# Linear attention and a maxout feed-forward: six of nine gate chunks in pairs by one level of Strassen

## The chip, the cores and the metric

The kernel runs on one core of a Trainium2 chip. The metric is the device time in microseconds (us) of that core; several executions are taken and their median is compared. The kernel before takes 719.25 us (median of 3 runs, 716.79 to 720.8).

The engines are TensorE (PE in the profile), VectorE (DVE), ScalarE (ACT), GpSimd (POOL) and SyncE (SP). Each runs its own instructions in order, and semaphores tie them together. SP only issues DMAs here; ACT issues a few as well.

## What is computed

q, k and v are (8, 8, 576, 64) in float32; x has 4608 rows (8 x 576 tokens) of 512 features (8 heads x 64). w1, w2 and w3 are 512 x 768 and w_out is 768 x 512, handed over as float64.

```python
q_s = exp(q - max(q, -1));  q_s = q_s / (sum(q_s, -1) + 1e-09)   # over a head's 64 features
k_s = exp(k - max(k, 2));   k_s = k_s / (sum(k_s, 2) + 1e-09)    # over the 576 tokens
kv = einsum('bhsd,bhse->bhde', k_s, v)
x  = einsum('bhsd,bhde->bhse', q_s, kv)      # then (tokens, 512)
h  = maximum(maximum(x @ w1, x @ w2), x @ w3)   # the gate product
out = h @ w_out                                 # the second product
```

## The kernel before

**Two parts of each number.** A product of two float32 matrices is made on PE from numbers cut into a high part (type float32r) and a low part, the remainder: high by high, high by low and low by high, three matmuls into one PSUM bank. Weights, x and the hidden layer h each exist in two parts: `wh` and `wl`, slot 0 and 1 of `xbuf`, `h_h` and `h_l`, `oh` and `ol` for w_out.

**Weights.** They come as 64-bit words and are joined to float32 on chip, 24 slices of 128 x 512 (`Slice`): load L332 into a slot `wst`, bit work on DVE (L344 to L351), a POOL addition (L355), the high part by ACT (L363), the low part by DVE or POOL (L370). A slot comes free when its low part is done.

**Heads.** One `Pair` is two heads of one batch (32 pairs). In batches 0 and 1 ("turned") q and k are transposed by PE, and x is one float32 matmul. In batches 2 to 7 q is read with rows in another order, normalised by DVE and ACT (L580 to L595), transposed in blocks by DVE (L600) and laid out by eight small DMAs on SP (L613), then cut in two parts (L619 ACT, L622 DVE). k's maximum is taken by three DVE steps (L481 to L483) and one POOL reduction (L486), then subtracted (L489) and exponentiated (ACT L496); k v is ten small matmuls (L511). Its block-diagonal matrix is written in two parts (`bdh` ACT L527, `bdl` DVE L531). x of a head pair (L663) is then three matmuls of 512 columns, and three of 64 columns for the last 64 tokens; its two parts are written by ACT (L666) and DVE (L668).

**Chunks.** Each batch's first 512 tokens are a chunk, and the eight last 64s together (`left`) a ninth. For a chunk the gate product (L693) is 18 groups (6 tiles j of 128 hidden features, 3 weights i) of 12 matmuls of 512 columns: 4 blocks of 128 features by the 3 terms, 216 in all, into 4 rotating PSUM banks (`pf`). After each group ACT copies it (L702) or DVE takes the maximum (L705); then h is cut in two (ACT L708, DVE L712). The second product (L732) is 4 groups of 18 matmuls; ACT copies each out (L750), SP stores it (L757). Heads' transposes and x use three banks `pa` and a bank of quarters `ps`.

**Order.** A planner (`Streams`) writes the order of every engine's instructions before the program is built: each piece of work is a chain of `Step`s with a cost, a rank, what it waits for and what rooms it takes and frees; the planner always issues the step that can begin first, by rank among those. The program then runs in this order on each engine.

Of the kernel before, what the change touches and what calls it, by code (L numbers as in the profile page):

```python
# [12 lines left out]
I32 = mybir.dt.int32  # L13
# [29 lines left out]
Q_BY_ACT = (0, 4, 6)  # L43

# [35 lines left out]
class Streams:  # L80
# [3 lines left out]
    def __init__(self, rooms, queued):  # L84
        self.all, self.when, self.blocked, self.left = [], {}, {}, 0
        self.queued = queued
        self.rooms = rooms
        self.taken = {}
        self.freed = {}
        self.clock = {"S": 0.72, "A": 2.2, "V": 4.0, "G": 9.0, "T": 0.0, "-": 0.0}  # L90
        self.port = 0.0
        self.queues = 0.0

    def add(self, gen, rank, inc=0.0):
        self.all.append([gen, rank, inc, 0.0, None, None])

    def ready(self, s, engine):
        step = s[4]
        lat = SIGNAL + (AHEAD if engine == "T" else 0.0)
        if engine == "-":  # L100
            t = s[3]
        elif s[5] != engine:
            t = s[3] + lat
        else:
            t = s[3] + 0.08 if engine not in "ST" else 0.0
# [6 lines left out]
        for r, key in step.take:  # L112
# [3 lines left out]
            if len(taken) >= self.rooms[r]:  # L116
# [52 lines left out]
    def issue(self, t, e, c, s):  # L169
# [9 lines left out]
        s[3], s[5] = end, e  # L179
# [5 lines left out]
        for r, key in step.take:  # L185
            self.taken.setdefault(r, []).append(key)
        for f in step.free:
            self.freed[f] = end
        s[1] += s[2]
# [6 lines left out]
def linear_attention_then_maxout_ffn(  # L196
# [46 lines left out]
    hp = ctx.enter_context(tc.tile_pool(name="hp", bufs=NJ))  # L243
    tmp = ctx.enter_context(tc.tile_pool(name="tmp", bufs=3))
    pf = ctx.enter_context(tc.tile_pool(name="pf", bufs=4, space=PSUM))
    pa = ctx.enter_context(tc.tile_pool(name="pa", bufs=3, space=PSUM))
# [4 lines left out]
    wh = [const.tile([P, NC, DF], F32R, name=f"wh{i}") for i in range(3)]  # L251
    wl = [const.tile([P, NC, DF], F32R, name=f"wl{i}") for i in range(3)]
    wo = []
    left = const.tile([P, 2, NC, B * LEFT], F32R, name="left")
    xbuf = [const.tile([P, 2, NC, CH], F32R, name="x0")]
# [5 lines left out]
    bdh, bdl = [], []  # L261
# [36 lines left out]

    in_pf = []
    for c in range(B + 1):  # L300
        in_pf += [(c, j, i) for j in range(NJ) for i in range(3)] + [(c, "y", t) for t in range(4)]
    st = Streams({"pf": 4, "pa": 3, "ps": 4, "keT": 1, "hp": NJ, "tmp": 3, "ke": 2, "qe": 2, "qf": 1, "qt": 2, "tb": 1, "qT": 2, "qhl": 1}, {"pf": in_pf})
    late_pools, turn_pools = [], []
# [6 lines left out]
    class Slice:  # L310


        def __init__(self, n):
            self.n = n
            if n < NG:
                j, i = divmod(n, 3)
                js = slice(j * P, (j + 1) * P)
                self.src = (w1, w2, w3)[i].bitcast(U32)[:, 2 * j * P : 2 * (j + 1) * P].rearrange("(c p) n -> p c n", p=P)
                self.parts = lambda: (wh[i][:, :, js], wl[i][:, :, js])
# [16 lines left out]
        def join(self, room):  # L336
# [17 lines left out]
            yield Step("G", 1.43, [("low", n)], gives=("w", n), port="G")  # L354
            nc.gpsimd.tensor_add(out=low.bitcast(I32), in0=x.bitcast(I32), in1=low.bitcast(I32))  # L355
# [9 lines left out]
        def lo(self, room):  # L365
# [4 lines left out]
            unit[e].tensor_sub(out=lo, in0=self.view(self.low.bitcast(F32)), in1=h.bitcast(F32))  # L370
# [3 lines left out]
    class Pair:  # L374
# [59 lines left out]
        def k_turned(self):  # L434
# [4 lines left out]
            kT = pa.tile([P, CH], F32, name="pa")  # L439
# [22 lines left out]
            kep = pa.tile([P, CH], F32, name="pa")  # L462
# [35 lines left out]
        def k_steps(self):  # L498
# [25 lines left out]
            yield Step("A", 0.65, free=last if turned else (), gives=("bd", n) if turned else None)  # L524
            for r in heads:
                to = (bdf if turned else bdh)[self.m]
                nc.scalar.activation(out=to[r, r], in_=kv[r, 0:D], func=AF.Copy, scale=rk[r])  # L527
            if not turned:
                yield Step("V", 0.45, free=last, gives=("bd", n))
                for r in heads:  # L530
                    nc.vector.scalar_tensor_tensor(  # L531
                        out=bdl[self.m][r, r],
                        in0=kv[r, 0:D],
                        scalar=rk[r],
                        in1=bdh[self.m][r, r].bitcast(F32),
                        op0=ALU.mult,
                        op1=ALU.subtract,
                    )


        def q_steps(self):
# [61 lines left out]
            for i in range(P // BL):  # L603
                for e in range(2):
                    end = i == P // BL - 1 and e == 1
                    yield Step(
                        "S", 0.6, take=[("qT", n)] if i == e == 0 else (), free=[("tb", n)] if end else (),
                        gives=("qT", n) if end else None, kb=36,
                    )
                    if i == e == 0:  # L610
                        self.qT = turn_pools[0].tile([P, S], F32, name="qT", bufs=2)
                    r = D * (i // 2) + BL * e
                    nc.sync.dma_start(  # L613
# [3 lines left out]
            yield Step("A", act(S), [("qT", n)], take=[("qhl", n)])  # L617
            q_h = turn_pools[0].tile([P, S], F32R, name="q_h", bufs=1)
            nc.scalar.copy(out=q_h, in_=self.qT)  # L619
            yield Step("V", dve(S), free=[("qT", n)], gives=("qhl", n), port="V")  # L620
            q_l = turn_pools[0].tile([P, S], F32R, name="q_l", bufs=1)
            nc.vector.tensor_sub(out=q_l, in0=self.qT, in1=q_h.bitcast(F32))  # L622
            self.terms = [(bdh[self.m], q_l), (bdl[self.m], q_h), (bdh[self.m], q_h)]

        def x_place(self, u):
            if u == 0:
                return tuple(xbuf[self.b % 2][:, i, self.g, :] for i in range(2))
            return tuple(left[:, i, self.g, self.b * LEFT : (self.b + 1) * LEFT] for i in range(2))

        def turned_steps(self):  # L630
# [3 lines left out]
            qT = pa.tile([P, CH], F32, name="pa")  # L634
# [11 lines left out]
            yield Step("A", act(LEFT), free=[("ps", ("qTl", n))], gives=("qhl", n))  # L646
            nc.scalar.copy(out=qf[:, CH:], in_=qTl[:, :LEFT])
            self.terms = [(bdf[self.m], qf)]

        def x_steps(self, u):  # L650
# [4 lines left out]
            cost = f32(w) if self.turned else 3 * f32r(w)  # L655
            after = [("bd", n), ("qhl", n), ("xmm", n, 0) if u else None]
            if u == 0:
                after += [("gates", b - 2) if b >= 2 else None, "late" if b == 1 else None]
            yield Step("T", cost, after, take=[room], gives=("xmm", n, u), free=[("qf" if self.turned else "qhl", n)] if u else ())
            xT = (next(small) if u else pa.tile([P, CH], F32, name="pa"))[:, :w]  # L660
            last = len(self.terms) - 1
            for i, (l, r) in enumerate(self.terms):
                nc.tensor.matmul(out=xT, lhsT=l, rhs=r[:, cs], start=(i == 0), stop=(i == last))  # L663
            h, lo = self.x_place(u)
            yield Step("A", act(w))
            nc.scalar.copy(out=h, in_=xT)  # L666
            yield Step("V", dve(w), free=[room], gives=("x", b, self.g) if u == 0 else ("xl", b, self.g))
# [4 lines left out]
    class Chunk:  # L672
# [6 lines left out]
        def gate(self, j, i):  # L679
            c, js = self.c, slice(j * P, (j + 1) * P)  # L680
            key = (c, j, i)
            for cc in range(NC):
                x = [("x", c, cc)] if c < B else [("xl", b, cc) for b in range(B)]
                yield Step(
                    "T", 3 * f32r(CH), [("split", 3 * j + i), *x], take=[("pf", key)] if cc == 0 else (),
                    gives=("gate", c, j, i) if cc == NC - 1 else None,
                )
                if cc == 0:
                    ps = pf.tile([P, CH], F32, name="pf")
                src = xbuf[c % 2] if c < B else left  # L690
                h, lo = src[:, 0, cc, :], src[:, 1, cc, :]
                for t, (l, r) in enumerate(((wl[i], h), (wh[i], lo), (wh[i], h))):
                    nc.tensor.matmul(  # L693
                        out=ps, lhsT=l[:, cc, js], rhs=r, start=(cc == 0 and t == 0), stop=(cc == NC - 1 and t == 2)
# [3 lines left out]
        def hidden(self, j):  # L698
# [8 lines left out]
            h = self.hh[j] = hp.tile([P, CH], F32R, name="h_h")  # L707
# [216 lines left out]
```

## Time and profile before

| | |
|---|---|
| median of 3 runs | 719.25 us (716.79 to 720.8) |
| profiled execution, span | 716.9 us |
| PE | busy 687.5 us, 3528 matmuls |
| DVE | busy 410.7 us, 819 instructions |
| ACT | busy 245.3 us, 529 instructions |
| POOL | busy 56.2 us, 70 instructions |
| DMA | 58.06 MB, mean 81 GB/s |
| HBM | 40.89 MB read, 9.44 MB written |
| L693, gate product | 1152 matmuls with a weight's high part and 576 with its low part in chunks 0 to 7; the ninth chunk's 216 have groups of their own |
| SP's longest wait | L757 for ACT at L750: 134.3 us in total, 9 times |

The profiled execution's span is 716.9 us; that is the time which the prediction's sum is made against, and the median stands 2.35 us above it. A row of the costliest groups reads: line, engine, operation, what is written and read, sizes, type, count, then busy time, mean ns of one, and idle time of the engine before them with what ended it. "PEld" is the loading of the stationary operand, which overlaps matmuls. In a row of the chain of waits stand start, length, engine, tile, line and count; in a row of the timeline start and length, then the instruction. Matmuls are pipelined, so that the mean of one overlaps its neighbours; the price of a matmul in a stream is the length of a stretch over its count.

### The profile page before, as it was taken

How to read it: one execution, taken by the hardware profiler on the slowest of the kernel's cores; microseconds unless marked ns; L12 is line 12 of the kernel's file. 1: busy time of each engine (PE TensorE's matmuls, PEld its weight loads, DVE VectorE, ACT ScalarE, POOL GpSimd, SP SyncE). 2: the span in 40 equal slices, each digit the busy share in tenths (PEclk: the TensorE clock that was granted, in tenths of full speed). 3: DMA queues.
4: the chain of work that ended last, by engine and by line, in shares of the span. 5: the costliest groups of instructions: out<-in, count | busy, mean ns of one | idle time of the engine just before them, and what ended most of it. 6: DMA issues, size and time to landing. Idle time of an engine off the chain costs nothing.

```text
span 716.9 us, 9773 instructions
## 1 busy us (share of the span) xinstructions
PE 687.5 (96%) x3528; PEld 553.2 (77%) x3528; DVE 410.7 (57%) x819; ACT 245.3 (34%) x529; POOL 56.2 (8%) x70
## 2 busy tenths in 40 slices
PE   2868999999999999999999999999999999999997
PEld 1536887778888888888888888887888888888885
DVE  7977978489996987785478546653422112211220
ACT  4677746433443334421342135113411111111111
POOL 3222332100000000000000001000000000000000
PEclk9959999999999999999999999999999999999999
DMA  9945713414453333530253015200200010010002
GB/s 232 246 129 160 218 46 106 125 29 121 117 155 102 99 93 101 148 85 17 59 152 98 16 43 160 76 13 26 84 1 0 16 45 0 1 44 16 1 0 59
DMA packets 86416, 58.06 MB, mean 81 GB/s; under 512 B 53344, under 2 KB 77920, under 8 KB 86368
## 3 DMA queue, kind: packets, MB, share of 16 engines
q1 hardware_dynamic: 86288, 57.31, 29.1%
q8 instruction: 28, 0.46, 0.3%
q14 instruction: 20, 0.16, 0.1%
q10 hardware_dynamic: 80, 0.13, 0.0%
HBM read 40.89 MB, written 9.44 MB: 70 GB/s over the span
## 4 chain that ended last, share of the span: by engine, by line
PE 92%; DVE 4%; DMA 2%; issue 1%; ACT 1%; SPq 1%; DVEq 0%; ACTq 0%
PE pf L693 62%; PE pf L732 21%; PE pa L663 3%; PE ps L511 3%; DMA wst<-in_moe_w_dram 2%; PE ps L663 1%; PE pa L636 1%; DVE wx L351 0%; DVE wx L346 0%; DVE wl L370 0%; PE pa L464 0%; SPq L795 0%; DVE km L450 0%; DVE qm L550 0%; DVE wx L347 0%
## 5 line engine op out<-in xcount | busy, mean ns | idle before, releaser
L693 PE MATMUL pf<-x,wh 128*128 128x512 f32 x1152 | 358.2, 392 | 0.0
L693 PEld LDWEIGHTS pf<-x,wh 128*128 128x128 f32 x1152 | 217.8, 189 | 46.4 <-issue 0.5
L693 PE MATMUL pf<-x,wl 128*128 128x512 f32 x576 | 230.3, 400 | 1.2 <-DVE wl L370 1.2
L705 DVE TENSOR_TENSOR m<-pf,m 128x512 f32<-128x512 f32 x108 | 74.6, 690 | 179.4 <-PE pf L693 176.3
L693 PEld LDWEIGHTS pf<-x,wl 128*128 128x128 f32 x576 | 108.8, 189 | 25.6 <-DVE wl L370 1.6
L708 ACT CAST h_h<-m 128x512 fp32r<-128x512 f32 x54 | 33.5, 620 | 187.4 <-DVE m L705 187.3
L732 PE MATMUL pf<-ol,h_h 128*128 128x512 f32 x216 | 88.5, 410 | 0.0
L732 PE MATMUL pf<-oh,h_l 128*128 128x512 f32 x216 | 84.5, 391 | 0.0
L732 PE MATMUL pf<-oh,h_h 128*128 128x512 f32 x216 | 84.3, 390 | 0.0
L702 ACT COPY m<-pf 128x512 f32<-128x512 f32 x54 | 31.7, 586 | 58.4 <-PE pf L693 57.5
L712 DVE TENSOR_TENSOR h_l<-m,h_h 128x512 fp32r<-128x512 f32 x54 | 37.2, 689 | 18.7 <-ACT h_h L708 18.5
L732 PEld LDWEIGHTS pf<-oh,h_l 128*128 128x128 f32 x216 | 40.5, 188 | 9.1
L732 PEld LDWEIGHTS pf<-ol,h_h 128*128 128x128 f32 x216 | 40.6, 188 | 8.7 <-issue 0.2
L732 PEld LDWEIGHTS pf<-oh,h_h 128*128 128x128 f32 x216 | 40.7, 188 | 7.7 <-issue 0.2
L693 PE MATMUL pf<-left,wh 128*128 128x512 f32 x144 | 44.3, 389 | 0.0
L486 POOL PARTITION_ALL_REDUCE kma<-km x24 | 17.8, 741 | 299.4 <-DVE ke L489 169.1
L668 DVE TENSOR_TENSOR x<-pa,x 128x512 fp32r<-128x512 f32 x32 | 22.0, 688 | 29.7 <-ACT x L666 29.7
L355 POOL TENSOR_TENSOR wst<-wx,wst 128x512 int32<-128x512 int32 x24 | 31.7, 1322 | 86.6 <-DVE wx L351 37.1
L750 ACT COPY m<-pf 128x512 f32<-128x512 f32 x35 | 20.4, 586 | 50.9 <-PE pf L732 49.2
L600 DVE STREAM_TRANSPOSE tb<-qt 128x576 f32<-128x576 f32 x24 | 30.8, 1285 | 3.5 <-DMA qT<-tb 3.0
L693 PEld LDWEIGHTS pf<-left,wh 128*128 128x128 f32 x144 | 27.0, 188 | 5.6
L666 ACT CAST x<-pa 128x512 fp32r<-128x512 f32 x32 | 18.8, 586 | 30.7 <-PE pa L663 30.6
(115 smaller groups left out, 676.5 us busy)
## 6 DMA issues: line engine op xcount, KB each, us to landing
wst<-in_moe_w_dram SPq DMA_DIRECT2D x18, 512.0 KB, 4.6
out_dram<-m SPq DMA_DIRECT2D x32, 256.0 KB, 2.3
vt<-in_v_dram SPq DMA_DIRECT2D x56, 128.0 KB, 2.9
qt<-in_q_dram SPq DMA_DIRECT2D x24, 288.0 KB, 3.0
qT<-tb SPq DMA_DIRECT2D x192, 36.0 KB, 1.9
kt<-in_k_dram SPq DMA_DIRECT2D x24, 256.0 KB, 3.0
wst<-in_moe_w_out_dram SPq DMA_DIRECT2D x6, 512.0 KB, 3.5
q<-in_q_dram SPq DMA_DIRECT2D x8, 256.0 KB, 3.5
```

Source lines behind the costliest of these rows:

```text
L355: nc.gpsimd.tensor_add(out=low.bitcast(I32), in0=x.bitcast(I32), in1=low.bitcast(I32))
L511: nc.tensor.matmul(out=kv[r, :nv], lhsT=ke[rows, s, hh, :], rhs=self.vt[rows, hh, s, 0:nv], start=(s == 0), stop=(s == 4),)
L600: nc.vector.transpose(out=tb.rearrange("p e (c s) -> p s e c", s=QS), in_=self.qt.rearrange("p s (e c) -> p s e c", e=2))
L663: nc.tensor.matmul(out=xT, lhsT=l, rhs=r[:, cs], start=(i == 0), stop=(i == last))
L668: nc.vector.tensor_sub(out=lo, in0=xT, in1=h.bitcast(F32))
L693: nc.tensor.matmul(out=ps, lhsT=l[:, cc, js], rhs=r, start=(cc == 0 and t == 0), stop=(cc == NC - 1 and t == 2))
L702: nc.scalar.copy(out=m, in_=self.m.pop((j, 0)))
L705: nc.vector.tensor_max(out=m, in0=self.m.pop((j, i)), in1=m)
L708: nc.scalar.copy(out=h, in_=m)
L712: unit[e].tensor_sub(out=lo, in0=m, in1=h.bitcast(F32))
L732: nc.tensor.matmul(out=po, lhsT=l, rhs=r[:, j, :], start=(j == 0 and i == 0), stop=(j == NJ - 1 and i == 2))
L750: nc.scalar.copy(out=o, in_=po)
```

## The change

Chunks 0 to 2 stay as they were (`PLAIN = 3`). Chunks 3 to 8 are taken in three pairs (`Duo`), and the gate product of a pair is made by one level of Strassen's scheme in Winograd's form: of x a 2 x 2 block matrix is made (two halves of the 512 features, two chunks), of the weights another (two tiles of 128 hidden features, two halves of the features), and a product of the two takes seven block products in place of eight.

- The 18 weight tiles are nine "functions" of two tiles each: three "apart" (w3, two j) and six "pair" (w1 and w2 of one j). Each has 7 products of 6 matmuls (2 feature blocks x 3 terms), 63 products and 378 matmuls per pair of chunks (L932), where two chunks had 432.
- Four of the seven left factors are sums of weight quarters (`sums`, L1094 to L1105, nine times: one load, four DVE steps of 256 columns, an ACT cast, one DVE step of 1024 columns, one store of 1 MB). They start from the whole weights, which are written to a scratch in DRAM (`whole`, 18 stores of 256 KB), and go back to a scratch, as do the three plain quarters (`kept`, 27 stores).
- Before each pair its 63 left factors of 256 KB come through a ring of 16 places (`ring_loads`, L913, on SP), which lies in the room of the gate weights once chunk 2 is done.
- Of x seven right factors are made per pair (`mixing`): three cast in two parts, four differences first; 1024 columns each on ACT and DVE (L869 to L880).
- A product starts a bank or adds to one. Where it adds to a bank whose earlier value is still to be read, it waits for that read (`("read", ...)`). `apart` (2 ACT, 5 DVE steps) and `pair` (2 ACT, 7 DVE steps) form the sums, the maximum and h in float32 (`hf`); `split` (L1019, L1021) cuts h in two parts, one eighth ahead of each group of the second product (L1043, as many matmuls as before).
- x of batches 2 to 7 is one float32 matmul (L740) of q and a float32 block matrix; q and the block matrix are no longer cut in two parts. x of batches 3 to 7 and the last 64s of all are copied by ACT in float32 (L743).
- q's block DMAs go to SP or ACT's queue (L694), with three buffers `qT`; the buffers of temporaries go from 3 to 7; a weight slot comes free after POOL's addition; seven PSUM banks are given out by name (`banks_of_gates`, `banks_of_heads`); heads of batches 5 to 7 get a late rank (`LATER`).

```diff
+PLAIN = 3
+RING = 16
+N_TMP = 7
+LEFT_OF = (0, 1, 6, 2, 3, 4, 5)
+MIX_OF = (0, 1, 4, 6, 2, 3, 5)
+KINDS = {
+    "apart": (
+        (0, "x", True), (5, "y", True), (4, "z", True), (1, "x", False), (6, "y", False), (3, "y", False), (2, "z", False),
+    ),
...
+        order += [(fa, a, n) for n in (1, 2, 3, 4)]
+        order += [(fb, b, 0), (fa, a, 5), (fb, b, 1), (fa, a, 6)]
...
+            nc.tensor.matmul(out=xT, lhsT=self.terms[0], rhs=self.terms[1][:, cs], start=True, stop=True)
+            if u or b >= PLAIN:
+                yield Step("A", act(w), free=[room], gives=("xl" if u else "x", b, self.g))
+                nc.scalar.copy(out=self.raw_place(u), in_=xT)
...
+        def mix_sum(self, m, to, in0, in1, after):
+            e = yield Step("VG", (dve(2 * CH), pool(2 * CH)), after, gives=("sum", self.c, m), port="VG")
+            full = self.raw(*to)
+            unit[e].tensor_sub(out=full, in0=self.raw(*in0), in1=self.raw(*in1))
+            yield Step("A", act(2 * CH), self.room_of(m))
+            nc.scalar.copy(out=self.parts(m, 0), in_=full)
+            yield Step("V", dve(2 * CH), gives=("mix", self.c, m), port="V")
+            nc.vector.tensor_sub(out=self.parts(m, 1), in0=full, in1=self.parts(m, 0).bitcast(F32))
...
+                after = [("scratch", f, a < 2, a == 2, a > 2)]
+                if k < RING:
+                    after += self.block_free(k * CH // NW)
+                yield Step("S", 0.64, after, take=[("ring", k)], gives=("ringed", k), kb=256)
+                nc.sync.dma_start(out=ring[k % RING].bitcast(F32).rearrange("p t a b -> p (t a b)"), in_=scratch[f, :, a, :])
...
+                after = [("ringed", k), ("mix", self.c, m)]
+                if not first:
+                    after.append(("read", self.c, f, bank, [x[1] for x in KINDS[kind][:n]].count(bank)))
+                w, x = ring[k % RING], mixes[m]
+                for cc in range(2):
...
+                    for t, (a, b) in enumerate(((1, 0), (0, 1), (0, 0))):
+                        nc.tensor.matmul(
+                            out=po, lhsT=w[:, a, cc], rhs=x[:, b, cc],
...
+            yield Step("V", dve(CH), done(1), take=[tile_of("u2")], gives=("read", c, f, "y", 1), rank=-1000.0)
+            u2 = tmp.tile([P, CH], F32, name="m")
+            nc.vector.tensor_add(out=u2, in0=po("y"), in1=s)
...
+            yield Step("V", dve(CH), done(4), take=[tile_of("u3")], gives=("read", c, f, "y", 2), rank=-1000.0)
```

What the planner makes of it shows at the passage from chunk 2 to the first pair. First PE, from the end of chunk 2's second product on; `ps` holds k v and narrow pieces of x, `ol` and `oh` are w_out's parts. Before:

```order
L511 MATMUL ps<-vt_93,ke 64x65 x10
L732 MATMUL pf<-ol,h_h 128x512
L732 MATMUL pf<-oh,h_h 128x512
L732 MATMUL pf<-oh,h_l 128x512
L693 MATMUL pf<-x_768,wl_82 128x512
L693 MATMUL pf<-x_768,wh_79 128x512 x2
```

And after; `gw` holds the ring and the mixes, and the banks have numbers:

```order
L812 MATMUL bank_81<-ol,h 128x512
L812 MATMUL bank_81<-oh,h 128x512 x2
L932 MATMUL bank_86<-gw 128x512 x6
L603 MATMUL ps<-vt_92,ke 64x65 x10
L603 MATMUL ps<-vt_93,ke 64x65 x10
L932 MATMUL bank_82<-gw 128x512 x6
L932 MATMUL bank_83<-gw 128x512 x6
L932 MATMUL bank_86<-gw 128x512 x6
L932 MATMUL bank_82<-gw 128x512 x6
L932 MATMUL bank_80<-gw 128x512 x6
L932 MATMUL bank_82<-gw 128x512 x6
```

Where chunk 3's gates began, the first pair's products now stand: five of function 0, one of function 1 into `bank_80`, one more of function 0, with two blocks of k v after the first product, and with repeated visits to `bank_86` and `bank_82`, each of which adds to a bank that was read in between.

Second DVE, up to the first step that reads what then comes out of PE (L705 and L959); `qm`, `qs` and `qt` are q's maxima, sums and rows, `kh` and `km` k's maxima. Before:

```order
L522 TENSOR_SCALAR rk<-ps 128x1
L523 RECIPROCAL rk<-rk 128x1
L489 TENSOR_TENSOR ke<-kt_91,kma 128x2x5x64
L481 TENSOR_TENSOR kh<-kt_90 128x256
L482 TENSOR_TENSOR km<-kh 128x128
L483 TENSOR_TENSOR km<-km,kt_90 128x128
L531 SCALAR_TENSOR_TENSOR bdl_1475<-ps,rk,bdh_1471 64x64 x2
L668 TENSOR_TENSOR x_86<-pa,x_86 128x512
L668 TENSOR_TENSOR left<-ps,left 128x64
L580 TENSOR_REDUCE qm_175<-qt 128x9
L705 TENSOR_TENSOR m<-pf,m 128x512
```

And after, where `raw` is x in float32 and `bench` holds the sums of weight quarters:

```order
L1099 TENSOR_TENSOR bench<-bench 128x256
L871 TENSOR_TENSOR gw<-raw,gw 128x1024
L880 TENSOR_TENSOR gw<-raw,gw 128x1024
L876 TENSOR_TENSOR raw<-raw 128x1024
L1099 TENSOR_TENSOR bench<-bench 128x256
L876 TENSOR_TENSOR raw<-raw 128x1024
L880 TENSOR_TENSOR gw<-raw,gw 128x1024
L1099 TENSOR_TENSOR bench<-bench 128x256
L880 TENSOR_TENSOR gw<-raw,gw 128x1024
L1099 TENSOR_TENSOR bench<-bench 128x256
L661 TENSOR_REDUCE qm_177<-qt 128x9
L959 TENSOR_TENSOR m<-bank_82,m 128x512
```

In place of heads' steps of 64 to 640 columns and of x's second parts, DVE has the differences of x (L876), the second parts of the mixes (L871, L880) and quarters' sums (L1099) ahead of its first read of a product.

Third SP's queue, beside the first pair's products. Before, around the first stores of chunk 3's output, it had heads' loads, q's block DMAs and those stores:

```order
L613 DMA qT<-tb 32x288 x4
L414 DMA vt_93<-in_v_dram 128x4x64 x2
L416 DMA vt_93<-in_v_dram 64x2x64
L757 DMA out_dram<-m 128x512
L403 DMA kt_91<-in_k_dram 128x2x256
L405 DMA kt_91<-in_k_dram 64x2x64
```

And after, while the first pair's products run:

```order
L913 DMA gw<-scratch 128x512
L694 DMA qT<-tb 32x288
L913 DMA gw<-scratch 128x512 x2
L506 DMA vt_93<-in_v_dram 128x4x64 x2
L508 DMA vt_93<-in_v_dram 64x2x64
L913 DMA gw<-scratch 128x512
L495 DMA kt_91<-in_k_dram 128x2x256
L497 DMA kt_91<-in_k_dram 64x2x64
```

The ring's loads (L913) now stand between the heads' loads and the block DMAs.

More of the change, by code (lines that the diff above doesn't have):

```diff
@@ L369, in lo, with whole @@
             h, lo = self.parts()
-            unit[e].tensor_sub(out=lo, in0=self.view(self.low.bitcast(F32)), in1=h.bitcast(F32))
+            unit[e].tensor_sub(out=lo, in0=self.view(self.full), in1=h.bitcast(F32))
+            if n < NG:
+                yield Step("-", 0.0, [("whole", n)], free=[("tmp", ("w", n))])
+        def whole(self):
+            n = self.n
+            f, i = next((f, duos[0].tiles_of(f).index(n)) for f in range(NG // 2) if n in duos[0].tiles_of(f))
+            yield Step("S", 0.64, [("w", n)], gives=("whole", n), kb=256)
+            nc.sync.dma_start(out=wholes[f, :, i, :], in_=self.full)
     class Pair:
@@ L523, in k_steps @@
             nc.vector.reciprocal(out=rk, in_=rk)
-            yield Step("A", 0.65, free=last if turned else (), gives=("bd", n) if turned else None)
+            yield Step("A", 0.65, free=last, gives=("bd", n))
+            to = (bdf if turned else bds)[self.m]
             for r in heads:
-                to = (bdf if turned else bdh)[self.m]
                 nc.scalar.activation(out=to[r, r], in_=kv[r, 0:D], func=AF.Copy, scale=rk[r])
[L528 to L538, printed above, removed]
         def q_steps(self):
@@ L616, in q_steps, with raw_place @@
                     )
[L617 to L625, printed above, removed]
+            self.terms = (bds[self.m], self.qT)
+        def raw_place(self, u):
             if u == 0:
-                return tuple(xbuf[self.b % 2][:, i, self.g, :] for i in range(2))
-            return tuple(left[:, i, self.g, self.b * LEFT : (self.b + 1) * LEFT] for i in range(2))
+                if not raws:
+                    raws.append(late_pools[1].tile([P, 2, NC, CH], F32, name="raw", tag="x1"))
+                return raws[0][:, (self.b - PLAIN) % 2, self.g, :]
+            return left[:, self.g, self.b * LEFT : (self.b + 1) * LEFT]
         def turned_steps(self):
@@ L688, in gate @@
                 if cc == 0:
[L689 to L692, printed above, removed]
+                    ps = banks[st.bank("pf", key)]
+                h, lo = (xbuf[c % 2][:, t, cc, :] for t in range(2))
+                for t, (l, r) in enumerate(((w_l, h), (w_h, lo), (w_h, h))):
                     nc.tensor.matmul(
-                        out=ps, lhsT=l[:, cc, js], rhs=r, start=(cc == 0 and t == 0), stop=(cc == NC - 1 and t == 2)
+                        out=ps, lhsT=l[:, cc], rhs=r, start=(cc == 0 and t == 0), stop=(cc == NC - 1 and t == 2)
                     )
@@ L891, in linear_attention_then_maxout_ffn @@
             st.add(ch.second(t), r + 50 + t)
+    for f in range(NG // 2):
+        st.add(kept(f), SUMS_AT + SUMS_STEP * f)
+        st.add(sums(f), SUMS_AT + SUMS_STEP * f)
+    for d, duo in enumerate(duos):
+        r = GATES_AT + 100.0 * (PLAIN + d)
+        st.add(duo.ring_loads(), r - 100.0)
+        for n, mix in enumerate(duo.mixing()):
+            st.add(mix, -900.0 + n)
+        st.add(duo.mixed(), 0.0)
+        st.add(duo.gates(), r)
+        for f in range(NG // 2):
+            st.add(duo.apart(f) if f % 3 == 0 else duo.pair(f), -1000.0)
+        st.add(duo.all_split(), 0.0)
+        for t in range(8):
+            st.add(duo.split(t), 0.0)
+            st.add(duo.second(t), r + 50 + t)
     with tc.manual_schedule():
```

403 lines of the change are left out of this document (339 added, 64 removed).

## The prediction

> **What bounds the kernel now.** I read the page first: the busy shares (part 1), the slices (part 2) and the shares of the chain that ended last (part 4).
>
> ```profile
> span 716.9 us, 9773 instructions
> PE 687.5 (96%) x3528; PEld 553.2 (77%) x3528; DVE 410.7 (57%) x819; ACT 245.3 (34%) x529; POOL 56.2 (8%) x70
> PEclk9959999999999999999999999999999999999999
> PE 92%; DVE 4%; DMA 2%; issue 1%; ACT 1%; SPq 1%; DVEq 0%; ACTq 0%
> PE pf L693 62%; PE pf L732 21%; PE pa L663 3%; PE ps L511 3%; DMA wst<-in_moe_w_dram 2%; PE ps L663 1%; PE pa L636 1%; DVE wx L351 0%; DVE wx L346 0%; DVE wl L370 0%; PE pa L464 0%; SPq L795 0%; DVE km L450 0%; DVE qm L550 0%; DVE wx L347 0%
> ```
>
> TensorE is the chain (92%), and 62% of the span is the gate product's line. But an average hides when the other engines are tight, so next I cut the span into stages: the start, chunks 1 to 3, chunk 5, chunk 7. The columns are busy time and count of PE, weight loads, DVE, ACT and POOL, then the granted clock, the DMA share and GB/s.
>
> ```profile
> 0.00:70.00 70.00, 45.51 (x260) 30.60 (x261) 56.02 (x131) 45.06 (x133) 19.12 (x26) 0.88 0.73 191
> 135.00:214.00 79.00, 79.00 (x446) 62.96 (x445) 64.85 (x141) 31.40 (x63) 7.20 (x9) 1.00 0.42 111
> 192.00:214.00 22.00, 22.00 (x132) 17.75 (x131) 20.74 (x50) 8.83 (x18) 2.11 (x3) 1.00 0.55 150
> 214.00:292.00 78.00, 77.70 (x447) 63.23 (x446) 59.70 (x123) 29.88 (x57) 4.21 (x6) 1.00 0.39 105
> 440.00:513.00 73.00, 73.00 (x390) 59.27 (x389) 39.99 (x77) 21.63 (x42) 1.70 (x2) 1.00 0.21 60
> 581.00:647.00 66.00, 66.00 (x290) 54.27 (x289) 12.45 (x18) 9.59 (x16) 0.00 (x0) 1.00 0.04 16
> ```
>
> From 70 us on PE has hardly an idle microsecond. VectorE is its close second as long as it prepares q and k: 82% busy in 135 to 214 (64.85 of 79), 94% in the tail of that (20.74 of 22), 77% in the next chunk, and 19% in chunk 7, when no heads are left. So fewer matmuls are worth their full time late in the kernel, and in the middle only as long as DVE keeps up.
>
> **The change part by part.** *Matmuls saved.* Before, nine chunks take 216 gate matmuls each. After, three chunks do, and each of the three pairs takes 63 products of 6 matmuls, 378 where 432 stood. PE's list of the new program holds just that (648 at L773, 1134 at L932, 648 in the second product as before), so the arithmetic is cut as the diff says: 162 matmuls. Their price is that of a whole chunk in the chain of waits, in order of time (start, length, line, count):
>
> ```profile
> 581.18 49.44 PE pf L693 x216
> 646.94 48.97 PE pf L693 x216
> ```
>
> 48.97 / 216 = 0.2267 us, so 162 are 36.7 us, all of it on the path. The Trainium skill, page "TensorE: Matmul & The Clock Gate", section "Back-to-back issue gap", puts the sustained price of a 512-column matmul in a stream of weight loads and matmuls at about 131 ns. By that, an estimate from the page, the gain would be 21.2 us and my time 15.5 us later; the trace has 227 ns over 216 in a row and decides.
>
> *x in float32.* For 24 head pairs three matmuls over two-part operands become one in float32, 512 and 64 columns wide. In the first pair of rows the three (0.69), in the second a float32 one as the two turned batches have it (0.86), from the chain; then the narrow ones from the timeline.
>
> ```profile
> 271.25 0.69 PE pa L663 x3
> 120.03 0.86 PE pa L663 x2
> 273.16 0.19 PE L663 MATMUL ps<-q_l,bdh 128*128 128x64 f32 x1
> 273.72 0.39 PE L732 MATMUL pf<-oh,h_h 128*128 128x512 f32 x1
> 121.98 0.33 PE L663 MATMUL ps<-qf,bdf 128*128 128x64 f32 x2
> 122.44 0.40 PE L732 MATMUL pf<-oh,h_h 128*128 128x512 f32 x1
> ```
>
> Each timeline stretch holds the narrow ones and one 0.23 us matmul: 0.56 - 0.23 = 0.33 before, 0.46 - 0.23 = 0.23 after. Sum: 24 x (0.17 - 0.10) = +1.7 us. PE alone would therefore end at 716.9 - 36.7 + 1.7 = 681.9 us. The rest is what PE newly waits for.
>
> *DVE's work.* Rows for its prices:
>
> ```profile
> L705 DVE TENSOR_TENSOR m<-pf,m 128x512 f32<-128x512 f32 x108 | 74.6, 690 | 179.4 <-PE pf L693 176.3 <-ACT qt L587 0.7 <-ACT wh L363 0.7
> L489 DVE TENSOR_TENSOR ke<-kt,kma 128x640 f32<-128x640 f32 x24 | 19.3, 803 | 0.6 <-POOL kma L486 0.6
> L481 DVE TENSOR_TENSOR kh<-kt 128x256 f32<-128x256 f32 x24 | 9.8, 409 | 0.3 <-DMA kt<-in_k_dram 0.2
> L600 DVE STREAM_TRANSPOSE tb<-qt 128x576 f32<-128x576 f32 x24 | 30.8, 1285 | 3.5 <-DMA qT<-tb 3.0 <-issue 0.3
> 212.75 0.16 DVE L523 RECIPROCAL rk<-rk 128x1 f32<-128x1 f32 x1
> 212.83 0.15 DVE L591 TENSOR_SCALAR qs<-qs 128x9 f32<-128x9 f32 x1
> ```
>
> From 256 to 640 columns DVE pays 1.03 ns a column, so a 1024-column mix is an estimated 1.2 us. The last two rows overlap by 0.08 us: instructions start before their forerunners end, and all groups of DVE add to 442 us where the page has 410.7 busy, so I scale sums of DVE rows by 0.93. With its order list priced so, the new program asks of DVE, between the same points of the program: 60 against 64 us before chunk 0's first maximum, 62 against 61 in chunk 0, 76 against 75 in chunk 1. Until there it is a draw: what the sums of weight quarters (nine times four of 256 columns and one of 1024, 25 us in all) add, the dropped second parts of x, q and the block matrix give back. Then DVE gets 55 us of rows in chunk 2's gates, 26 from its last gate to the first product, 95 beside the first pair's products. From chunk 1 on that is 252 x 0.93 = 234 us of work in 255.5 us of PE's (PE's own list by the prices above: 78.8 chunk 1, 77.2 chunk 2, 99.5 the products with their heads). 92% is less than the 94% that DVE reached, but more than its 82% over a whole chunk.
>
> *First wait: mixing x for pair one.* The second product needs x mix 3, the difference of two half chunks, which needs the last gate of chunk 2 out of the buffer. DVE's list puts 23.6 us of rows between that chunk's last maximum and this mix; x 0.93 = 21.9, at the 94% above 23.3, plus 0.3 to start. PE has the second product (72 x 0.2267 = 16.3), two x (2.2), product one (1.4) and two blocks of k v (1.5, at 0.73 each in the chain): 21.4. So it waits about 2.2, and with ACT's casts in between I take 3. Ends: 0 if DVE is ahead, 7.6 if it runs at the 77% of chunk 2.
>
> *Returns into banks.* A product that adds to a bank waits until DVE or ACT has read it. Nine times per pair only one other product, 6 x 0.2267 = 1.36 us, lies between. The trip, from the timeline of chunk 7 (last gate matmul, then the maximum that waited for it):
>
> ```profile
> 594.29 0.62 PE L693 MATMUL pf<-x,wh 128*128 128x512 f32 x2
> 595.01 0.69 DVE L705 TENSOR_TENSOR m<-pf,m 128x512 f32<-128x512 f32 x1 [3.48 <-PE pf L693]
> ```
>
> The second of those matmuls starts at 594.52 and gives way at 594.75; DVE starts 0.26 later and ends after 0.69. With 0.1 back and a weight load ahead (0.2), that is 1.25, covered by 1.36 if DVE is free. In pairs two and three it is (no heads remain): 0.5 us for both, ends 0 and 4. Beside pair one heads stand on DVE too: 9 x 0.4 = 3.6; ends 0 and 9 x 1.285, a transpose in front each time, 11.6.
>
> *DMA.* The pairs stream 63 x 256 KB each through a ring of 16, about 140 GB/s over some 118 us. Writes of whole 2 KB rows reached 47 GB/s at a share of 0.13 in the first row below, hence some 360 at full share: hidden, and 16 products are 22 us of lead. SP's issue is 0.6 to 0.7 (next rows, two and one): 156 of them beside pair one are some 100 us of 138. In the start, though, 12 MB of weights are written back between about 40 and 112 us, where the share is already near one half; weight slots come free a step earlier, which helps. I take +1, ends -2 and +5.
>
> ```profile
> 564.00:581.00 17.00, 17.00 (x76) 14.06 (x75) 1.38 (x2) 2.38 (x4) 0.00 (x0) 1.00 0.13 47
> 211.88 1.40 SPq L414 DMA_DIRECT2D vt<-in_v_dram  x2
> 213.38 0.62 SPq L416 DMA_DIRECT2D vt<-in_v_dram  x1
> ```
>
> Sum: 681.9 + 1 + 3 + 3.6 + 0.5 = 690.0 us of span. The median of the runs shown, 719.25, stands 2.35 above the profiled span (the runs go from 716.79 to 720.8), so I predict 690.0 + 2.35 = 692.
>
> **The rivals.** *DVE sets the pace until pair one is done.* If it keeps only an 85% share from chunk 1 on, its 234 us take 275, 19.8 over PE's 255.5, in place of my 3 + 3.6: 681.9 + 1 + 19.8 + 0.5 + 2.35 = 706; at the 82% of 135 to 214 it is 716. It decides below 92%. For it: in-order waits on ACT, POOL and loads kept DVE at 77 to 82% over whole chunks; against: it had no more to do there, and reached 94% where it had. Chance 0.18.
>
> *SP's queue is late.* Ring loads share it with heads, transposes by DMA and sums that wait for DVE; whatever stands behind a waiting one waits. If its 156 issues beside pair one cost 0.95 us each with their waits, they take 148 us, 10 over PE's 138: 702. For it: SP waited 134 us for ACT at one line before, against: those were waits for the end of work. Chance 0.07.
>
> *Slower: the returns are never covered.* A pair has 30 returns into banks (four in each of three functions, three in each of six), 90 in all. If PE idles over 0.39 us at each, the 35 us saved are gone; with one more 512-column DVE or ACT step in front (0.69 less the 0.11 of slack, 0.58) they cost 52: 681.9 + 1 + 3 + 52 + 2.35 = 740. Against: 63 of the 90 have two or more products between, 2.7 us. The same page of the Trainium skill, section "A second HAM failure mode: psum-queue depth-cycling", tells of a kernel whose short idling between groups kept tripping the clock gate, which speaks for this rival; here the granted clock was 1.00 in every stage after 70 us, and 0.88 only where PE was busy 45.51 of 70. Chance 0.10.
>
> **How the numbers follow.** My own case has 0.65. Its bounds: 681.9 - 2 + 2.35 = 682 below; 681.9 + 5 + 7.6 + 11.6 + 4 + 2.35 = 712 above, which takes in the queue and most of the DVE rival. Outside lie 0.10 of slower and some 0.06 of the rest: the range is 682 to 712. Within 0.5% (about what a measurement of this kernel can tell from no change) lies only DVE's upper end, 0.04; slower 0.10; faster 0.65 + 0.07 + 0.14 = 0.86.
>
> **What would show it.** In the changed profile: 1134 matmuls at L932 and a span per pair near 121 us in pairs two and three (378 and 144 x 0.2267 = 118); idle time before L932 of a few us, at the first pair and ended by DVE; DVE at 90% or more until then. I am wrong if L932's idle time runs through all three pairs, if ring loads end it, or if a matmul there takes other than 0.227 us from start to start.

## The result and the profile after

The changed kernel takes 709.77 us (median of 5 runs, 706.54 to 711.94) where the kernel before takes 719.27 us beside it (716.79 to 721.18): a ratio of 0.986 (95% interval 0.983 to 0.989). It is faster by 9.5 us, where 27 were forecast; the time lies inside the stated range, at its slow end. The profiled execution has a span of 704.7 us, against the 690.0 of the sum. It is the quickest of the five (706.54 us), 3.2 us under the median, so below the differences of medians stand beside those of spans where it matters.

From the page of the changed kernel: span, busy shares, PE's and the DMA engines' slices, the DMA total, and the chain that ended last.

```profile
span 704.7 us, 9928 instructions
PE 656.3 (93%) x3318; PEld 516.6 (73%) x3318; DVE 480.6 (68%) x865; ACT 264.1 (37%) x548; POOL 57.5 (8%) x68
PE   2859999999999788989988999999999999999997
DMA  9999984416668976778878883346666316665012
DMA packets 126162, 133.57 MB, mean 190 GB/s; under 512 B 57376, under 2 KB 88864, under 8 KB 124960
PE 73%; DMA 13%; DVE 6%; SPq 4%; ACT 2%; issue 1%; ACTq 0%; DVEq 0%
```

PE is busy 31.2 us less than before, but idle 48.4 us (704.7 - 656.3) where it was 29.4. The holes are in slices 14 to 22 (a slice is 17.6 us), in which the DMA engines now stand at 6 to 9 tenths, and the chain has 13% of DMA where it had 2%. Bytes moved went from 58.06 to 133.57 MB: 75.5 MB pass through the scratch.

Six stages, cut at their first matmuls: chunk 1's gates, chunk 2's gates, chunk 2's second product, the first pair's products, all of pair two, all of pair three. Columns as in the prediction: busy time and count of PE, weight loads, DVE, ACT and POOL, granted clock, DMA share, GB/s.

```profile
134.20:193.95 59.75, 59.75 (x339) 46.56 (x338) 48.59 (x98) 23.09 (x46) 5.59 (x7) 1.00 0.54 157
214.56:287.71 73.15, 64.56 (x337) 48.69 (x336) 54.02 (x104) 27.34 (x51) 3.11 (x4) 0.93 0.76 236
287.71:306.44 18.73, 18.73 (x82) 14.73 (x81) 17.40 (x32) 9.23 (x15) 1.77 (x2) 1.00 0.80 252
306.44:418.56 112.12, 102.36 (x566) 78.94 (x564) 93.79 (x171) 39.27 (x76) 6.00 (x8) 1.00 0.80 234
463.90:581.73 117.83, 117.83 (x520) 96.94 (x519) 58.88 (x78) 29.32 (x47) 0.00 (x0) 1.00 0.54 157
581.73:700.30 118.57, 118.57 (x523) 97.81 (x521) 46.93 (x67) 21.42 (x36) 0.00 (x0) 1.00 0.43 122
```

Pairs two and three run as forecast, with PE busy throughout. The loss is in two stages: chunk 2's gates (73.15 us, 8.6 of them idle and the clock at 0.93) and the first pair's products (112.12, 9.8 idle). DVE is at 74% and 84% there, so it does not seem to set the pace; experiment 1 tests that. What PE waited for, over the whole span (us in total, times, longest; the rows of the start are left out):

```profile
PE bank L740 <- DMA qT<-tb: 11.9, 7, 3.8
PE bank L740 <- DMA gw<-scratch: 3.4, 1, 3.4
PE bank L932 <- ACT gw L878: 1.1, 1, 1.1
PE bank L932 <- DVE gw L880: 1.0, 1, 1.0
PE bank L932 <- DVE m L1000: 0.8, 1, 0.8
```

The products (L932) hardly wait, for the mixes 2.1 us and for a bank 0.8. It is the x matmul (L740) that waits, for q's block DMAs (`qT<-tb`), and PE's in-order list stands behind it. (L740 reads nothing of the ring; a row with `gw<-scratch` there names the landing that the profile saw last.) The chain of waits in chunk 2's gates, in order of time:

```profile
220.98 1.20 DVE tb L681
...
223.29 0.57 SPq L913
223.90 6.06 DMA gw<-scratch
229.98 0.56 SPq L694
230.59 2.38 DMA qT<-tb
232.97 0.24 issue
233.21 2.05 PE bank L740 x2
...
251.60 4.08 DMA qT<-tb
...
256.05 1.25 DVE tb L681
257.32 6.26 DMA qT<-tb
263.61 0.51 SPq L694
264.16 1.91 DMA qT<-tb
266.07 0.20 issue
266.27 2.05 PE bank L740 x2
```

From the block transpose to x it takes 12 us the first time (220.98 to 233.21) and 10 the second. A ring load of 256 KB that no product needs for another 80 us (the first runs at 306) lies in the way of q's blocks of 36 KB: the chain puts the issue of a block at 229.98 down to its landing, and that at 263.61 to the landing of an earlier block. Between the two, the next transpose waits for the only buffer `tb`. The blocks themselves land later too. Number, size and median time from issue to landing, the first row before, on SP alone; then after, of ACT's and of SP's queue:

```profile
qT<-tb SPq DMA_DIRECT2D x192, 36.0 KB, 1.9
qT<-tb ACTq DMA_DIRECT2D x109, 36.0 KB, 3.4
qT<-tb SPq DMA_DIRECT2D x83, 36.0 KB, 2.8
```

A wait costs more than its length. The first three rows are PE's timeline around three waits at L740, the last three the stretches right behind them (granted clock in the third column from the end):

```profile
233.21 2.05 PE L740 MATMUL bank<-qT,bd 128*128 128x512 f32 x2 [3.79 <-DMA qT<-tb]
266.27 2.05 PE L740 MATMUL bank<-qT,bd 128*128 128x512 f32 x2 [2.63 <-DMA qT<-tb]
363.55 1.10 PE L740 MATMUL bank<-qT,bd 128*128 128x512 f32 x2 [3.39 <-DMA gw<-scratch]
233.00:237.00 4.00, 3.79 (x7) 2.40 (x8) 3.12 (x11) 1.79 (x4) 0.00 (x0) 0.50 1.08 264
266.20:270.00 3.80, 3.73 (x8) 2.35 (x9) 3.80 (x5) 1.71 (x3) 0.00 (x0) 0.57 0.84 245
363.50:367.00 3.50, 3.45 (x14) 2.59 (x15) 3.37 (x6) 1.29 (x3) 0.00 (x0) 1.00 0.90 265
```

After the waits of 3.79 and 2.63 us the granted clock was 0.50 and 0.57 for some 4 us, and the x matmul took 2.05 us in place of 1.10; after 3.39 us it stayed at 1.00. The Trainium skill, page "TensorE: Matmul & The Clock Gate", section "HAM oscillation — how this bites in real kernels", says that idle gaps of PE above about 3.4 us halve its clock. The longest gap here agrees, the one of 2.63 us does not; here the measurement decides.

### The profile page after: what moved, and what is told of

It reads as the page before. It is cut to its first block, busy times and chain, and to the rows that moved or that the text cites. A ratio compares the mean times of both kernels' runs of the same rounds, so it can differ in the third digit from the quotient of the medians.

```text
span 704.7 us, 9928 instructions
## 1 busy us (share of the span) xinstructions
PE 656.3 (93%) x3318; PEld 516.6 (73%) x3318; DVE 480.6 (68%) x865; ACT 264.1 (37%) x548; POOL 57.5 (8%) x68
## 2 busy tenths in 40 slices
DMA packets 126162, 133.57 MB, mean 190 GB/s; under 512 B 57376, under 2 KB 88864, under 8 KB 124960
## 4 chain that ended last, share of the span: by engine, by line
PE 73%; DMA 13%; DVE 6%; SPq 4%; ACT 2%; issue 1%; ACTq 0%; DVEq 0%
PE bank L932 33%; PE bank L773 18%; PE bank L1043 10%; DMA qT<-tb 6%; PE bank L812 4%; PE bank L740 3%; PE ps L603 2%; DMA wst<-in_moe_w_dram 2%; DVE tb L681 1%; DMA qt<-in_q_dram 1%; DMA vt<-in_v_dram 1%; DVE gw L880 1%; SPq L694 1%; DMA gw<-scratch 1%; DVE raw L876 1%
## 5 line engine op out<-in xcount | busy, mean ns | idle before, releaser
L932 PE MATMUL bank<-gw 128*128 128x512 f32 x1134 | 268.6, 395 | 3.0 <-ACT gw L878 1.1
L932 PEld LDWEIGHTS bank<-gw 128*128 128x128 f32 x1134 | 211.6, 188 | 51.6 <-issue 4.6
L773 PE MATMUL bank<-gw 128*128 128x512 f32 x432 | 112.6, 414 | 0.0
L773 PEld LDWEIGHTS bank<-gw 128*128 128x128 f32 x432 | 82.5, 195 | 21.5 <-issue 4.5
L1043 PE MATMUL bank<-oh,halves 128*128 128x512 f32 x288 | 89.2, 390 | 0.8 <-DVE halves L1021 0.8
L1043 PEld LDWEIGHTS bank<-oh,halves 128*128 128x128 f32 x288 | 54.1, 188 | 13.0 <-DVE halves L1021 1.2
L1043 PE MATMUL bank<-ol,halves 128*128 128x512 f32 x144 | 57.4, 398 | 0.0
L773 PE MATMUL bank<-x,gw 128*128 128x512 f32 x216 | 53.8, 403 | 0.0
L773 PEld LDWEIGHTS bank<-x,gw 128*128 128x128 f32 x216 | 40.1, 188 | 10.0 <-issue 1.4
L812 PE MATMUL bank<-oh,h 128*128 128x512 f32 x144 | 44.8, 393 | 0.0
L1021 DVE TENSOR_TENSOR halves<-hf,halves 128x768 fp32r<-128x768 f32 (+2 forms) x30 | 23.8, 798 | 30.1 <-ACT halves L1019 30.1
L740 PE MATMUL bank<-qT,bd 128*128 128x512 f32 x48 | 27.2, 650 | 15.8 <-DMA qT<-tb 11.9
L785 DVE TENSOR_TENSOR m<-bank,m 128x512 f32<-128x512 f32 x36 | 24.7, 686 | 11.4 <-PE bank L773 10.8
L1062 ACT COPY m<-bank 128x512 f32<-128x512 f32 x23 | 13.5, 586 | 48.9 <-PE bank L1043 40.1
L1043 PEld LDWEIGHTS bank<-ol,halves 128*128 128x128 f32 x144 | 27.0, 188 | 6.1 <-ACT qt L668 0.2
L989 ACT COPY m<-bank 128x512 f32<-128x512 f32 x18 | 10.5, 586 | 55.5 <-PE bank L932 45.4
L994 ACT COPY m<-bank 128x512 f32<-128x512 f32 x18 | 10.6, 587 | 55.3 <-PE bank L932 54.5
L996 DVE TENSOR_TENSOR m<-bank,m 128x512 f32<-128x512 f32 x18 | 12.4, 690 | 25.5 <-PE bank L932 21.4
```

Source lines behind the costliest of these rows:

```text
L740: nc.tensor.matmul(out=xT, lhsT=self.terms[0], rhs=self.terms[1][:, cs], start=True, stop=True)
L773: nc.tensor.matmul(out=ps, lhsT=l[:, cc], rhs=r, start=(cc == 0 and t == 0), stop=(cc == NC - 1 and t == 2))
L785: nc.vector.tensor_max(out=m, in0=self.m.pop((j, i)), in1=m)
L812: nc.tensor.matmul(out=po, lhsT=l, rhs=r[:, j, :], start=(j == 0 and i == 0), stop=(j == NJ - 1 and i == 2))
L932: nc.tensor.matmul(out=po, lhsT=w[:, a, cc], rhs=x[:, b, cc], start=(first and cc == 0 and t == 0), stop=(cc == 1 and t == 2), skip_group_ ...
L996: nc.vector.tensor_sub(out=ma, in0=po("w"), in1=ma)
```

## The experiments

Theories: **A**, the bytes of the scratch (stores, sums, ring loads) keep the DMA engines busy, so that q's block DMAs land late. **B**, the single buffer `tb` makes a loop of transpose and eight DMAs that is too long in itself. **C**, the block DMAs are issued late: in SP's queue behind loads, or in ACT's, where they take ACT's time. "Same order" below means that every engine's instructions but the edited DMAs stand where they stood in the changed kernel.

**1. All scratch transfers at 16 of their 128 rows.** Same order. The expectation speaks of 86 MB; by the page it is 75.5. An eighth of the bytes still moves, and POOL has one memset more in the start.

```diff
-nc.sync.dma_start(out=ring[k % RING].bitcast(F32).rearrange("p t a b -> p (t a b)"), in_=scratch[f, :, a, :])
+nc.sync.dma_start(out=ring[k % RING].bitcast(F32).rearrange("p t a b -> p (t a b)")[0:16], in_=scratch[f, 0:16, a, :])
...
-nc.sync.dma_start(out=wholes[f, :, i, :], in_=self.full)
+nc.sync.dma_start(out=wholes[f, 0:16, i, :], in_=self.full[0:16])
...
+nc.gpsimd.memset(bench[0][:, 4 * CH :], 0.0)
```

> Every transfer to and from the scratch (whole weights, plain quarters, sums, ring loads) moves 16 of its 128 rows, an eighth of the bytes; the number of DMAs and the order of all instructions stay, and one 1024-column memset on POOL is added so that the sums' input is defined. The result is no longer the reference's, since the weights of the pairs are incomplete. Theory A, traffic: q's block DMAs come late because the scratch's 86 MB fill the DMA engines; then PE's waits at L740 for q (15.3 us in the changed kernel) fall below 3 us, chunk 2's gates go from 73.2 us to about 59, the first pair's products from 112.1 to about 102, and the span from 704.7 to 681-687 us. Theory B, one buffer for the transposed block: span 698-704. Theory C, the place of the DMAs in the queues of SP and ACT: span 697-704, with PE's waits at L740 still above 10 us.

684.17 us, ratio 0.952 (0.948 to 0.955), span 680.7. No wait at L740 for q's blocks is left. The same two stages as above:

```profile
213.40:273.00 59.60, 59.60 (x337) 46.41 (x336) 53.55 (x104) 27.22 (x51) 3.11 (x4) 1.00 0.52 129
291.70:395.50 103.80, 101.63 (x565) 79.17 (x564) 93.78 (x172) 39.78 (x76) 6.00 (x8) 1.00 0.44 117
```

Chunk 2's gates take 13.6 us less, the pair's products 8.3 less. The span is 24.0 us shorter (25.6 by the medians). PE is busy 649.8 us and idle 30.9, so of the 24.0 us that the bytes cost, 17.5 are waiting and 6.5 are PE's busy time; 5.0 of these are in chunk 2's gates, where the same 337 matmuls now run at a clock of 1.00 in place of 0.93. DVE reaches 90% in both stages (53.55 of 59.60, 93.78 of 103.80). The blocks' median falls from 3.4 to 2.4 us on ACT's queue and from 2.8 to 2.1 on SP's. SP also waits less for ring loads to land before it issues a block. The first row is the changed kernel, the second this run, both over the whole span:

```profile
SPq L694 <- DMA gw<-scratch: 8.5, 6, 3.6
SPq L694 <- DMA gw<-scratch: 1.0, 1, 1.0
```

So the bytes cause the loss in both stages, as theory A has it. That the blocks land later and that SP issues them later both go away with the bytes; this run does not tell how much each is worth.

**2. The ring loads alone at 16 of 128 rows.** Same order; only the first edit above. In 1 to 3 most of the pairs' weights are left out, so only the time counts.

> Only the ring loads (48 of the 86 MB) move 16 of 128 rows; all else and the order stay. The result is not the reference's. Theory A: the waits beside the first pair's products go (112.1 to about 103 us), those in chunk 2, where 1 MB stores of the sums run too, go by half (73.2 to about 66): span 686-692. Theories B and C: 700-705.

690.5 us, ratio 0.960 (0.958 to 0.962), span 688.6: the ring loads cost 16.1 us, the stores and sums the other 7.9 (19.3 and 6.3 by the medians). The pair's products take 103.9 us, as in experiment 1; chunk 2's gates 65.2, where the sums' stores of 1 MB still run.

**3. The ring loads with all 128 rows, 256 bytes of each.** Experiment 2 cuts rows together with the bytes; this one keeps all rows. Same order.

```diff
-nc.sync.dma_start(out=ring[k % RING].bitcast(F32).rearrange("p t a b -> p (t a b)"), in_=scratch[f, :, a, :])
+nc.sync.dma_start(out=ring[k % RING].bitcast(F32).rearrange("p t a b -> p (t a b)")[:, 0:64], in_=scratch[f, :, a, 0:64])
```

> As the run with thin ring loads, but each load keeps its 128 rows and moves 256 bytes of each instead of 2 KB: the same bytes as there (an eighth), eight times its rows. The result is not the reference's. If the bytes in the engines' way make q's blocks late: span 686-692, as there (688.6). If it is the number of packets that stand before them: 699-705, near the changed kernel's 704.7. In between it is some of each.

692.25 us, ratio 0.962 (0.960 to 0.964), span 690.9. Of the 16.1 us, 13.8 come back though all rows are there: it is the bytes, and hardly the number of rows.

**4. A second buffer `tb`.** Same order; the planner is left to believe in one.

```diff
-tb = turn_pools[0].tile([P, 2, BL * QS], F32, name="tb", bufs=1)
+tb = turn_pools[0].tile([P, 2, BL * QS], F32, name="tb", bufs=2)
```

> A second buffer for the transposed block (tb), with the planner left to believe in one, so that no engine's order changes. Theory B: the transpose no longer waits for the eighth block DMA of the pair before; the waits at L740 fall to some 5 us and the span to 692-697. Theory A: DVE's waits at L681 (7.0 us) go, but the block DMAs take as long as before; span 701-704. Theory C: 702-705.

702.97 us, ratio 0.977 (0.974 to 0.980), span 700.7, 4.0 us shorter (6.8 by the medians): just past what theory A allowed, and far from what theory B asked for. Waits for the blocks at L740 are still 10.2 us. The loop over one buffer is a part of the loss, and not the main one.

**5. All block DMAs on SP, and 6. all on ACT.** Order of the rest kept; the edit of 5 is shown, that of 6 has `nc.scalar` instead.

```diff
-(nc.sync if queue == "S" else nc.scalar).dma_start(
+nc.sync.dma_start(
```

> All of q's block DMAs are issued by SP at the places where the planner put them (109 were ACT's); the order of the other instructions stays. Theory C: if ACT's time in issuing (0.5 to 0.8 us each) makes exponentials and so q late, the span falls to 695-700; if the place behind SP's loads is what makes them late, it rises to 710-720. Theories A and B: within 3 us of 704.7, to either side.

> All of q's block DMAs are issued by ACT (83 were SP's) at the places where the planner put them. SP alone cost 14 us. If that was the place behind ring loads and sums in SP's order, ACT alone is faster than the mixture: 697-702. If ACT's time counts (83 more issues at 0.6 us are 50 us of an engine that is 37% busy, and exponentials stand behind them), it is slower: 707-715.

On SP alone 720.28 us, ratio 1.001 (0.999 to 1.003), span 718.9; on ACT alone 726.94, ratio 1.010 (1.009 to 1.012), span 725.4. What PE waited for, in the first row on SP alone, then on ACT alone:

```profile
PE bank L740 <- DMA qT<-tb: 20.2, 12, 3.8
```

```profile
PE bank L740 <- DMA gw<-scratch: 8.4, 2, 4.9
PE bank L740 <- ACT bd L619: 5.6, 2, 4.3
PE ps L603 <- ACT left L743: 3.9, 5, 1.4
```

So theory C is true in both its forms, as a sensitivity: behind SP's loads the blocks come later still, and on ACT they hold up what else ACT does (`bd` at L619, the copies at L743). On SP alone the blocks' median from issue to landing is 2.5 us, shorter than in the mixture, so what makes them later there is their issue. ACT alone lies even beyond the 707 to 715 us that were expected of it. The mixture that the change makes is worth 14 to 21 us of span, 10.5 and 17.2 by the medians. The Trainium skill, page "DMA: Bandwidth & Descriptors", section "Issuing engines are not separate DMA queues", says that DMAs from all issuers share the same 16 engines, so that issuing from several saves only issue time, usually little. The first half agrees with experiment 1, where thinner transfers on SP's queue also made the blocks of ACT's queue land sooner (2.4 us in place of 3.4); that the saving is usually little does not hold here, where the choice of the queue was worth 10.5 us and more.

**7. The first 16 ring loads late, and 8. this with a second `tb`.** They are issued during chunk 2's second product instead of its gates; only SP's order changes. `load` issues one ring load.

```diff
+                if k < RING:
+                    held.append(load)
...
+                if c == PLAIN - 1 and held:
+                    held.pop(0)()
```

> The first 16 ring loads (4 MB) are issued one by one between the steps of chunk 2's second product instead of during chunk 2's gates; the order on PE, DVE and ACT stays, only SP's changes, and no byte is saved. Theory A (bytes in the way of q's block DMAs): chunk 2's gates go from 73.2 us to about 66, as where these loads were thin (65.2), and if nothing is late in the second product, where there are only two x, the span goes from 704.7 to 696-699. Rival: the loads only move the loss, q's blocks for the first pair come late instead, and the span stays at 701-706.

> The late first ring loads and the second buffer for the transposed block together, orders as in the two alone. If they act on different waits, their gains add: 704.7 less 4.0 (second buffer, measured) less what the late loads gain alone, 692-696. If both only take slack out of the same chain, no better than the better of the two.

713.91 us, ratio 0.991 (0.990 to 0.993), span 714.0; with the second buffer 713.65, ratio 0.992 (0.989 to 0.994), span 710.4. Both are slower than the change as it is, by 4.1 and 3.9 us of the medians, and beyond all that was expected of the first. Chunk 2's gates fell to 64.7 us, as theory A had it, but its second product took 28.6 in place of 18.7 and the pair's products 119.4 in place of 112.1. SP's timeline in the second product, then a step of DVE and one of PE that waited for the blocks:

```profile
294.02 0.43 SPq L916 DMA_DIRECT2D gw<-scratch  x1
294.50 0.55 SPq L694 DMA_DIRECT2D qT<-tb  x1
295.09 0.58 SPq L916 DMA_DIRECT2D gw<-scratch  x1
295.72 1.15 SPq L694 DMA_DIRECT2D qT<-tb  x2
```

```profile
300.04 1.20 DVE L681 STREAM_TRANSPOSE tb<-qt 128x576 f32<-128x576 f32 x1 [7.75 <-DMA qT<-tb]
300.05 2.05 PE L740 MATMUL bank<-qT,bd 128*128 128x512 f32 x2 [6.93 <-DMA qT<-tb]
```

Ring loads now stand between the blocks. The rival, that the loss only moves, was right about the place, and the loss grew by the move: a transfer that is harmless by its own deadline cost time where a chain of short DMAs ran.

**9. The planner reckons 3 us from issue to landing in place of 2.** Its estimate of a DMA (`DMA_LANDS`) sets the order.

```diff
-DMA_LANDS = 2.0
+DMA_LANDS = 3.0
```

> The planner reckons 3 us from a DMA's issue to its landing where it reckoned 2 (measured medians: 3.4 us for q's blocks on ACT's queue, 2.8 on SP's, 1.9 in the kernel before). All orders change. If the waits at L740 come from an order that was planned for short DMAs, PE finds other work in those gaps: 694-700. If the heads' chain itself is too slow with these DMAs, the order can't help: 701-708.

712.93 us, ratio 0.991 (0.988 to 0.993), span 709.5, beyond both expectations. The pair's products fell to 102.9 us, but the start lost 20 us: chunk 0's second product begins at 131.5 in place of 112.0, with a single wait of 10.1 us at L713 for DVE.

**10. to 14. A longer landing after 112 us only, and a second `tb`.** The planner's clock decides when; the buffer is unknown to it in the first three (3, 4 and 5 us), planned in the last two (4 and 3.5 us).

```diff
-end = self.queues + DMA_LANDS
+end = self.queues + (DMA_LANDS if begun < 112.0 else 4.0)
```

> The planner reckons 2 us of landing until its clock is at 112 us and 3 us after, so that the start keeps its order (reckoning 3 everywhere cost the start 20 us: 131.5 instead of 112.0 at chunk 0's second product, but made the first pair's products 102.9 instead of 112.1); the second tb buffer is there, unknown to the planner. If the order of the middle is what was planned too tight, span 690-697; if the start's order was only bad luck of the planner and the middle gains nothing by it, 700-704.

> As the run before with 4 us after 112 us, longer than the medians of 2.8 to 3.4: more slack between q's blocks and x. If slack is what counts, 688-696, at or below the run with 3; if the heads' chain is now planned too slow, so that x comes late by plan, 697-706.

> 5 us after 112 us. Beyond what the DMAs take in the median; if slack still pays, below the run with 4; if the plan is now too slow, 3 to 10 us above it.

> 4 us after 112 us, and the planner knows of the second tb buffer, so that the next transpose may stand before the eighth block DMA. If one buffer holds the planned chain back, 686-694, below the run where it is unknown; else within 3 us of it.

> 3.5 us of landing after 112 us with the second tb buffer planned, between the median (2.8 to 3.4) and the 4 us with which the span was 698.0 and the median 695.6. If planning with the real landing time is what helped, 692-698; if that run was a lucky order among many, 698-705.

| landing after 112 us | second `tb` | median us | ratio (interval) |
|---|---|---|---|
| 3 | not planned | 707.28 | 0.982 (0.978 to 0.986) |
| 4 | not planned | 703.30 | 0.978 (0.975 to 0.980) |
| 5 | not planned | 702.93 | 0.977 (0.974 to 0.980) |
| 4 | planned | 695.62 | 0.968 (0.964 to 0.972) |
| 3.5 | planned | 701.64 | 0.975 (0.973 to 0.977) |

None of the first three beats the second buffer in the old order (702.97): with 5 us chunk 2's gates fell to 64.4 us and the pair's products rose to 119.8, where PE's longest wait is now 7.2 us at L932 for a mix of x (L878). What one stage won, the next lost. Planned with two buffers and 4 us, the kernel takes 695.62 us, 14 less than the change and 24 less than before, the best order found; its neighbour with 3.5 us takes 701.64, in the range that was to mean a lucky order among many. So at least part of the 695.62 is luck, and how much stays open.

## Why the prediction was right in its direction and wrong in size

**The matmuls saved: right.** Pairs two and three stream at the old price, as the chain shows; 354 products' matmuls in 80.32 us are 0.2269 us each:

```profile
467.48 80.32 PE bank L932 x354
```

Without the scratch's bytes PE is busy 649.8 us, 37.7 less than before, where the sum had 36.7 - 1.7 = 35.0.

**The first wait: right.** 3 us for mixing x were forecast; at the first pair L932 waited 1.1 for ACT and 1.0 for DVE.

**Returns into banks: too dear.** 3.6 + 0.5 us were forecast and 0.8 is what the list of waits shows. The rival in which they are never covered fell with it.

**DVE: right, with little to spare.** The sum needed 92% of DVE from chunk 1 on; in experiment 1 it runs at 90% in the two tight stages, and PE is idle 2.2 us in them. The rival in which DVE sets the pace is refuted by that run, since DVE's instructions and order are the same there.

**The DMAs: wrong, and with them the size.** The step that failed is "hidden, and 16 products are 22 us of lead", with +1 us for the writes in the start. It asked whether the ring would be in time for its own readers, and it was. It did not ask what 75.5 MB do to the other DMAs: q's blocks went from a median of 1.9 us to 3.4 and 2.8, eight of them stand between a transpose and PE's x, and PE's list has that x in the middle of its products. Experiment 1 puts the price at 24.0 us of span where 1 stood. The other terms together were too high by 8.3 us (689.0 against the 680.7 of that run; the matmuls and the returns make up most of it), and so the span missed by 23.0 - 8.3 = 14.7. The rate was too good as well: from 47 GB/s at a share of 0.13 came some 360 at full share, while the rows of pairs two and three (157 at 0.54, 122 at 0.43) give an estimated 284 to 291. The start was nearly right: chunk 0's second product begins at 112.0 us, 1.1 later than in experiment 1.

That the time still lies inside the range is mostly luck. Its upper end of 712 was made of 5 us for the writes in the start and of waits for mixing and returns (7.6, 11.6 and 4), and of those waits 2.9 came; what filled the range was the wait for q's blocks, which none of its terms priced.

**The rival of SP's queue, at 0.07, came nearest** in place and size: 10 us beside the first pair were worked out and 8.3 were lost there. Its mechanism was half of it: SP does hold blocks back behind ring loads, and the issue order matters (experiments 5 to 7), but without the bytes the same order costs little, and chunk 2's gates, where it put nothing, lost more. The 706 us of the DVE rival lie closer to the measured time, for a cause that experiment 1 rules out.

## What to carry to other kernels

A stream of large transfers is not hidden because it is in time for its own readers: look for chains of short DMAs with an in-order engine at their end, and price what the stream adds to each of their links. Before moving such a stream, ask which chain runs where it would go; here the move cost more than it saved. When a wait in the profile is for a DMA, cut the bytes of the suspects at unchanged order: order and buffers stay, and what the traffic costs shows in one run, with the issues that waited for it.

## What the runs showed of the hardware

A block DMA of 36 KB between two places of the SBUF took a median of 1.9 us from issue to landing before, with a DMA share of 0.30 to 0.38 in the middle of the kernel; 2.1 to 2.4 us in experiment 1, with 0.44 to 0.53; and 2.8 to 3.4 us after the change, with 0.76 to 0.80. These shares are means of whole stages; right behind the three waits shown they stood at 0.84 to 1.08, and these runs do not show from which share on a block slows. And after a wait of 2.63 us, 10 us behind one of 1.41, PE's clock was granted at 0.57 for 3.8 us, but not after one of 3.39 us; what decides between them is not settled by these runs.
